# Attention, soft MoE and FFN in one kernel: four more half loads of v, a second feature tile converted early, five unused products

## The chip, the cores and the metric

One core of one Trainium2 chip runs the whole program in a single launch. The metric is the device time of one execution in microseconds (us), the median of several runs.

## The reference

Three layers follow each other. The first is windowed attention over 4 batches, 8 heads, 576 positions of 64 dimensions: the first four heads see the last 32 positions, the others every fourth of the last 128. The second is a soft mixture of 8 experts with 4 slots each, over all 2304 tokens. The third is a feed-forward layer (FFN) of 2048 features with a leaky gate; its weights arrive as 64-bit floats.

```python
scores = np.where(mask, scale * (q @ k.T), -1e9)
x = softmax(scores) @ v                            # then (B*S, H*D) = 2304 x 512
logits = x @ phi                                   # 2304 x 32
slot_input = softmax(logits, axis=0).T @ x         # 32 slots
slot_out[e] = np.maximum(slot_input[e] @ w1[e], 0) @ w2[e]
x = softmax(logits, axis=1) @ slot_out
h = x @ w_in                                       # 2304 x 2048
out = (np.maximum(h, 0) + alpha * np.minimum(h, 0)) @ w_out
```

## The kernel before

**Attention.** A unit is a pair of heads of one batch; there are 16 units (`u`), four for each batch. Each unit has nine blocks of 64 queries, and eight blocks in a row make a group (`g`), so 18 groups run through one pipeline: scores on TensorE (PE) into PSUM (`emit_s`, L360), maximum and subtraction on VectorE (DVE; L371, L374), exp on ScalarE (ACT; L377), sum and reciprocal on DVE, the scaling on GpSimd (POOL; `emit_norm`, L390), a transpose on PE (L395), its eviction by ACT or DVE, the product with v on PE (`emit_pv`, L408) and its eviction into `xt`. Behind it follow the logits (L440), transposes of x (L481) and the partial slot inputs (L490), batch by batch.

**The loads of v.** A block needs 64 keys in two overlapping layouts, so `v_m` holds v twice: rows 32 to 95 hold 64 rows, and rows 0 to 31 and 96 to 127 hold the same data shifted by one block. `load_v` (L332) brings all 128 rows (576 KB), or, for the units in `COPIED`, rows 32 to 95 alone (288 KB). For those, four tasks `vc` (`emit_vc`, L336) copy 32 rows each, on POOL (L342, a product with ones), ACT (L424) or DVE (L426); `emit_pv` of these blocks waits for them.

**Who sets the order.** `tasks_of_attention` (L508) lists the tasks with their needs, and `schedule` (L148) runs a list planner with costs from `COST` 2500 times with shaken keys and keeps the best order; tasks made with `either` may go to several engines. So another set of tasks gives another order on all engines. The FFN is planned in the same way (1500 rounds). Attention's tail (L647 to L695) and the experts (L816 to L853) are written out by hand.

**Loads.** All large loads are issued by SyncE (SP) in program order; a load waits for its place to be free, and what is behind it waits too. `plan` (L233) lists the loads of the expert weights (`a` for w1, `b` for w2, 1 or 2 MB each) and of the FFN's feature tiles; `order` (L216) names the place of each. Twelve places of 1 MB (`w0` to `w11`) are free from the start and are filled during attention. The next ones are `q_m`, `ep_m` and `v_m`, attention's own buffers, which come free when its scores (`q_m`) or its last product with v (`ep_m`) are done. After that each pair of places is loaded again when an expert has used it. Of feature tile 0, `w_in`'s half (`i`, 512 KB) is loaded ahead of the last expert's second matrix, and `w_out`'s half (`o`) behind it; feature tiles 1 to 15 (`f`) are loaded whole, 1 MB each.

**Feature tiles.** A tile is 128 features: 512 columns of w_in and 512 of w_out, as pairs of 32-bit words. `conv` (L789) makes a 32-bit float of each pair: step 0 on ACT (L796), steps 1 to 4 on DVE (L798, L800, L803, L806), then w_out is split into a high part (step 5, L424 or L426) and a low part (step 6, L813). Tile 0's w_in half is converted during the experts (L845), its w_out half as tasks `d0` to `d4` of the FFN; tiles 1 to 15 are converted whole as tasks `c0` to `c6`.

**The FFN.** `m1` and `m2` (L901, L978) multiply the slots' output with w_in, ACT (`ms`, `mp`) and DVE (`m3`, L906) make `mpack` of it; `h_` (L912) multiplies it with the packed softmax of the tokens (`cpack`), 384 tokens at a time. Then ACT takes relu (L1016), DVE the gate (L920), ACT the high part (`ghs`), POOL the low part (`gls`, L1022), and PE three products into `y` (L926): high by high, low weight by high, high by low. `VISITS` (L32) orders the work over three ranges of 768 tokens so that few features are needed at first: range 0 with feature 0, range 1 with features 0 and 1, range 2 with 0 to 2, and so on. After each visit ACT or DVE evicts six tiles of `y`.

`warm` (L503) issues products that nobody reads; `st` is the transposed output of the experts, `soT` its copy.

## Time and profile before

| what | us |
|---|---|
| median of 3 runs | 379.26 (378.06 to 381.27) |
| the profiled execution | 377.96 |
| its span, first to last instruction | 376.2 |
| PE, DVE, ACT, POOL busy | 357.4, 264.2, 216.6, 158.3 |

Everything that is read from a trace belongs to the profiled execution. Its time exceeds its span by 1.76 us, and the median of the runs lies 1.30 us above it. Attention's products end at 86 us, its tail at 94.7, the experts at 134, and the FFN's first product into `y` starts at 142.7. A busy PE is not PE at its peak, since matmuls overlap and their ends are modelled.

### The profile page before, as it was taken

To read this page: it belongs to the slowest core of one execution; us is meant where nothing else is said; L and a number is where in the kernel's file an instruction comes from. 1 tells how busy PE (TensorE), PEld (TensorE's weight loads), DVE (VectorE), ACT (ScalarE), POOL (GpSimd) and SP (SyncE) were. 2 spreads that over 40 slices of the span, in tenths; PEclk is the share of its full clock that TensorE was granted. 3 is DMA by queue.
4 is the path that set the end of the run, shared out by engine and by line. 5 is a ranking of instruction groups with operands and counts; after the bars stand their busy time and mean duration, and the time that the engine had idled before them with its cause. 6 is when DMAs were issued, how large, how long until landed. Compare 5 with 4: busy or idle time off the path is not lost.

```text
span 376.2 us, 7864 instructions
## 1 busy us (share of the span) xinstructions
PE 357.4 (95%) x3103; PEld 267.9 (71%) x3104; DVE 264.2 (70%) x455; ACT 216.6 (58%) x467; POOL 158.3 (42%) x145
## 2 busy tenths in 40 slices
PE   8699999998999878899999999999999999999995
PEld 3577777865444255677778778888888877888884
DVE  4979889875167349999999989898885224224263
ACT  2578969663122249878784956656556445535450
POOL 8336645320000005635655456574636424633550
PEclk9999999999999999999999999999999999999999
DMA  7999999999999993332333333110000000003246
GB/s 279 406 420 404 367 400 401 413 419 426 425 427 421 412 426 159 112 113 112 112 114 112 112 113 112 37 77 0 3 1 1 2 0 0 2 0 113 56 142 193
DMA packets 14036, 73.74 MB, mean 196 GB/s; under 512 B 1936, under 2 KB 2592, under 8 KB 9136
## 3 DMA queue, kind: packets, MB, share of 16 engines
q1 hardware_dynamic: 12736, 71.80, 48.7%
q10 hardware_dynamic: 1200, 1.38, 1.1%
q8 instruction: 24, 0.39, 0.4%
q14 instruction: 12, 0.10, 0.1%
q0 software_dynamic: 64, 0.07, 0.1%
HBM read 68.53 MB, written 4.72 MB: 195 GB/s over the span
## 4 chain that ended last, share of the span: by engine, by line
PE 71%; DMA 12%; DVE 8%; ACT 3%; POOL 2%; issue 2%; SPq 0%; DVEq 0%; POOLq 0%; ACTq 0%
PE y L926 45%; DMA w<-w 6%; PE pv L408 4%; PE hb L912 4%; PE s L360 3%; PE x L481 2%; PE si L490 2%; DMA v_m<-v 2%; PE h L724 2%; DMA q_m<-qk 2%; PE t L395 2%; DVE ep_m L803 2%; PE o L746 2%; PE lt L440 1%; DVE gs L920 1%
## 5 line engine op out<-in xcount | busy, mean ns | idle before, releaser
L1022 POOL TENSOR_TENSOR gls<-gs,ghs 128x384 fp32r<-128x384 f32 x96 | 116.0, 1223 | 162.9 <-ACT ghs L424 112.1
L926 PE MATMUL y<-wo_hi,ghs 128*128 128x512 f32 x289 | 90.8, 398 | 1.1 <-ACT ghs L424 0.9
L920 DVE SCALAR_TENSOR_TENSOR gs<-gs,beta_s,hb 128x384 f32<-128x384 f32 x96 | 56.4, 609 | 49.2 <-ACT gs L1016 45.8
L926 PE MATMUL y<-wo_hi,gls 128*128 128x512 f32 x289 | 87.5, 392 | 1.0 <-POOL gls L1022 1.0
L926 PE MATMUL y<-wo_lo,ghs 128*128 128x512 f32 x289 | 88.4, 392 | 0.0
L1016 ACT ACTIVATE gs<-hb 128x384 f32<-128x384 f32 x96 | 44.8, 494 | 45.5 <-PE hb L912 39.0
L926 PEld LDWEIGHTS y<-wo_hi,gls 128*128 128x128 f32 x289 | 54.1, 188 | 13.0 <-POOL gls L1022 1.7
L926 PEld LDWEIGHTS y<-wo_hi,ghs 128*128 128x128 f32 x289 | 53.3, 188 | 13.5 <-ACT ghs L424 2.4
L424 ACT CAST ghs<-gs 128x384 fp32r<-128x384 f32 x96 | 48.9, 517 | 22.5 <-DVE gs L920 21.8
L926 PEld LDWEIGHTS y<-wo_lo,ghs 128*128 128x128 f32 x289 | 54.0, 188 | 10.3
L390 POOL TENSOR_TENSOR ep_m<-ep_m,l 128x512 f32<-128x512 f32 x18 | 19.0, 1063 | 31.0 <-DVE l L386 16.2
L912 PE MATMUL hb<-cpack,mpack 128*128 128x384 f32 x96 | 29.2, 341 | 1.7 <-DVE mpack L906 1.1
L798 DVE TENSOR_SCALAR ep_m<-ep_m 128x1024 f32<-128x1024 f32 (+1 forms) x17 | 18.0, 1059 | 10.4 <-ACT ep_m L796 10.4
L360 PE MATMUL s<-q_m 128*64 128x64 f32 x576 | 20.8, 224 | 2.1 <-DVE l L381 1.5
L360 PEld LDWEIGHTS s<-q_m 128*64 128x64 f32 x576 | 18.6, 138 | 5.8 <-ACT q_m L424 2.9
L912 PEld LDWEIGHTS hb<-cpack,mpack 128*128 128x128 f32 x96 | 17.9, 188 | 6.3 <-DVE mpack L906 1.3
L408 PE MATMUL pv<-ep_m,v_m 128*64 128x64 f32 x576 | 20.2, 224 | 0.1
L424 ACT COPY ep_m<-t 64x512 f32<-64x512 f32 x34 | 19.7, 580 | 0.9 <-PE t L395 0.3
L408 PEld LDWEIGHTS pv<-ep_m,v_m 128*64 128x64 f32 x576 | 18.2, 138 | 2.7 <-issue 2.3
L800 DVE TENSOR_SCALAR ep_m<-ep_m 128x1024 int32<-128x1024 int32 (+1 forms) x17 | 16.7, 984 | 0.2
L727 ACT ACTIVATE v_m<-h,rinv 128x256 f32<-128x256 f32 x8 | 3.8, 474 | 20.7 <-PE h L724 20.7
L377 ACT ACTIVATE ep_m<-ep_m 128x512 f32<-128x512 f32 x18 | 11.4, 631 | 7.6 <-DVE ep_m L374 7.3
(149 smaller groups left out, 490.7 us busy)
## 6 DMA issues: line engine op xcount, KB each, us to landing
w<-w SPq DMA_DIRECT2D x14, 1024.0 KB, 8.6
w<-w SPq DMA_DIRECT2D x5, 2048.0 KB, 15.5
q_m<-qk SPq DMA_DIRECT2D x13, 576.0 KB, 6.6
q_m<-w_f SPq DMA_DIRECT2D x7, 1024.0 KB, 4.9
v_m<-w_f SPq DMA_DIRECT2D x7, 1024.0 KB, 4.8
v_m<-v SPq DMA_DIRECT2D x12, 576.0 KB, 6.7
q_m<-w SPq DMA_DIRECT2D x2, 2048.0 KB, 15.0
ep_m<-w SPq DMA_DIRECT2D x1, 2048.0 KB, 10.0
```

The source lines that it names most:

```text
L360: mm(s[r:r + 64, col:col + 64], lhsT=q_of(u)[:, 2 * o:2 * o + 64], rhs=keys(u, c, x), start=False, stop=True, skip_group_check=True)
L377: nc.scalar.activation(out=es[g % 4], in_=es[g % 4], func=AF.Exp, scale=SCALE)
L390: nc.gpsimd.tensor_tensor(out=e, in0=e, in1=bc(e_[g, "l"], 128, 8, 64), op=ALU.mult)
L408: mm(pv[hs, n], lhsT=vv[u % 4][:, c, hs], rhs=pts[:, NBS * (g % 2) + n, h], start=True, stop=True, skip_group_check=True)
L424: nc.scalar.copy(out=out, in_=in_)
L798: nc.vector.tensor_scalar(out=t, in0=t, scalar1=2.0 ** -15, scalar2=FMAX, op0=ALU.max, op1=ALU.min)
L800: nc.vector.tensor_scalar(out=ti, in0=ti, scalar1=3, scalar2=0x3FFFFFFF, op0=ALU.logical_shift_left, op1=ALU.bitwise_and)
L912: mm(hb[i], lhsT=mpack[:, 128 * f:128 * f + 128], rhs=cpack[:, t0:t0 + 384], start=True, stop=True)
L920: nc.vector.scalar_tensor_tensor(out=g, in0=g, scalar=beta_s[:, f:f + 1], in1=hb[i], op0=ALU.mult, op1=ALU.add)
L926: mm(y[steps[s][0], t][:, sl], lhsT=g, rhs=wo_hl[p == 1][:, f, sl], start=start, stop=stop, skip_group_check=True)
L1016: lambda s=s, i=i: nc.scalar.activation(out=half(gs, s, i, 4), in_=hb[i], func=AF.Relu, scale=-1.0),
L1022: lambda s=s, i=i: nc.gpsimd.tensor_tensor(out=half(gls, s, i, 6), in0=half(gs, s, i, 4), in1=half(ghs, s, i, 6).bitcast(F32), op=ALU.subt ...
```

## The change

Eight units instead of four (3, 4, 6, 7, 8, 10, 11, 12) load rows 32 to 95 of v and have the other rows copied: 16 more copies, four more loads of 288 KB in the place of 576 KB. Feature tile 1 is treated like tile 0: its w_in half (512 KB) is loaded ahead of the last expert's second matrix, into `xs`, and converted during the experts, its w_out half is loaded behind that matrix and converted in the FFN by the half-size steps. Three calls of `warm` in attention's tail issue five products that nobody reads.

```diff
--- before.py
+++ after.py
@@ -58,10 +58,11 @@
             c6=14, warm=60, pb=8)
 NST = HP * NC // 2
 NQ, NXT = 4, 7
-COPIED = (4, 6, 8, 10)
+COPIED = (3, 4, 6, 7, 8, 10, 11, 12)
 QZ = 2 * S
 KP = 2 * S + WIN
 NW = 12
+EARLY = (0, 1)
 
 
 def constants():
@@ -213,7 +214,7 @@
     slots = {"xs": xs_m[:, 0:2048]}
     for n, m in pairs.items():
         slots.update({n: m[:, 0:2048], second[n]: m[:, 2048:]})
-    order = [f"w{i}" for i in range(NW)] + ["q0", "q2", "e", "v0"] + ["w0", "w2", "w4", "w6", "w8", "q0", "w10", "w11", "q0", "xs", "q3", "v0", "v1"] + 3 * ["q2", "q3", "v0", "v1"]
+    order = [f"w{i}" for i in range(NW)] + ["q0", "q2", "e", "v0"] + ["w0", "w2", "w4", "w6", "w8", "q0", "xs", "w10", "w11", "q0", "xs", "q3", "v0", "v1"] + 3 * ["q2", "q3", "v0", "v1"]
 
     eye_s = const.tile([128, 128], F32, name="eye_s")
     sel_s = const.tile([128, 128], F32, name="sel_s")
@@ -235,9 +236,9 @@
         plan += [("a", e, x) for x in ((0, 1) if e < 4 else (2,))]
         if e > 0:
             plan += [("b", e - 1, x) for x in ((0, 1) if e < 3 else (2,))]
-    plan += [("i", 0, 0), ("b", NE - 1, 0), ("b", NE - 1, 1), ("o", 0, 0)]
-    FB = len(plan) - 1
-    plan += [("f", c, 0) for c in range(1, NF)]
+    plan += [("i", f, 0) for f in EARLY] + [("b", NE - 1, x) for x in range(2)]
+    FB = len(plan)
+    plan += [("o" if f in EARLY else "f", f, 0) for f in range(NF)]
     wt = {}
 
     def load_one(i):
@@ -664,6 +665,7 @@
         emit_dexp(b)
         x_(2, "act")
         emit_dT(b)
+        warm(2, tail[3][:, 128:256])
         emit_dTe(b)
         g1, g2 = small("g1", 1, 96), small("g2", 1, NS)
         nc.vector.tensor_reduce(out=g2, in_=j1[0:1, 0:96].rearrange("p (j s) -> p s j", j=3), op=ALU.min, axis=AX.X)
@@ -672,6 +674,7 @@
         emit_lts(b)
         emit_lrun(b)
         emit_part(b, 0)
+        warm(1, tail[3][:, 128:256])
         j2 = tail[1]
         mm(j2[0:96, 0:1], lhsT=g1, rhs=one_s, start=True, stop=True)
         gm, fac, lf = small("gm", 96, 1), small("fac", 96, 1), small("lf", 96, 1)
@@ -684,6 +687,7 @@
         emit_acc(b)
         j3 = tail[2]
         mm(j3[:, 0:1], lhsT=sel_s[0:96, :], rhs=lf, start=True, stop=True)
+        warm(2, tail[3][:, 128:256])
         used["xs"] = True
         load_weights()
         j4 = tail[3]
@@ -842,8 +846,9 @@
 
         yacc = [part(q_m, i, DM) for i in range(7)] + [part(xs_m, i, DM) for i in range(6)]
         yacc += [acc_m, v_m[:, 4096:4608]] + [part(m_m, i, DM) for i in range(3)]
-        for i in range(5):
-            conv(0, i, 0)
+        for f in EARLY:
+            for i in range(5):
+                conv(f, i, 0)
         emit_l2(NE - 1, 1)
         nc.scalar.copy(out=os, in_=o)
         warm(2, st[:, 256:384])
@@ -960,19 +965,14 @@
 
         for f in range(NF):
             k = when[f]
-            if f > 0:
-                landed = [("c4", x) for x in NEXT if NEXT[x] == f and x > 0]
-                for i in range(7):
-                    need = {0: landed + [dep("c6", f - 4), dep("m1", f - 4)], 5: [("c4", f)], 6: [("c5", f)]}
-                    task((f"c{i}", f), "act" if i in (0, 5) else "dve", lambda f=f, i=i: conv(f, i),
-                         need.get(i, [(f"c{i - 1}", f)]), k - LEAD[f"c{i}"], f"c{i}",
-                         2.6 * f + 1.6 if f < 6 else 0.0)
-            else:
-                for i in range(5):
-                    task((f"d{i}", 0), "dve" if i else "act", lambda i=i: conv(0, i, 1), [dep(f"d{i - 1}", 0)], -40, f"d{i}")
-                task(("c5", 0), "dve", lambda: conv(0, 5), [("d4", 0)], -40, "c5")
-                task(("c6", 0), "dve", lambda: conv(0, 6), [("c5", 0)], -2, "c6", 3.0)
-            task(("m1", f), "pe", lambda f=f: m1(f), [dep("c4", f), dep("ms", f - 1)], k - LEAD["m1"])
+            early = f in EARLY
+            landed = [("c4", x) for x in NEXT if NEXT[x] == f and x > 0] + [dep("c6", f - 4), dep("m1", f - 4)] if not early else []
+            for i in range(7):
+                kind = f"d{i}" if early and i < 5 else f"c{i}"
+                task((f"c{i}", f), "act" if i == 0 or i == 5 and f else "dve", lambda f=f, i=i: conv(f, i, 1 if f in EARLY and i < 5 else None),
+                     [(f"c{i - 1}", f)] if i else landed, (-40, -2)[i > 5] if f == 0 else k - LEAD[f"c{i}"], kind,
+                     3.0 if (i, f) == (6, 0) else 0.0 if early else 2.6 * f + (0 if 1 in EARLY else 1.6) if f < 6 else 0.0)
+            task(("m1", f), "pe", lambda f=f: m1(f), [None if f in EARLY else ("c4", f), dep("ms", f - 1)], k - LEAD["m1"])
             task(("ms", f), "act", lambda f=f: copy("act", ms[:, f % 2], mb[0]), [("m1", f), dep("m2", f - 2)],
                  k - LEAD["ms"])
             task(("m2", f), "pe", lambda f=f: mm(mb[1], lhsT=sel_s, rhs=ms[:, f % 2], start=True, stop=True),
```

On SP, at the end of attention and in the experts, the loads stand as follows before (w_84 is the pair of places w10 and w11, which takes the last expert's second matrix).

```order
L251 DMA q_m<-w 128x4096 x2
L251 DMA ep_m<-w 128x4096
L251 DMA v_m<-w 128x4096
L251 DMA w_79<-w 128x4096
L251 DMA w_80<-w 128x4096
L251 DMA w_81<-w 128x4096
L251 DMA w_82<-w 128x4096
L251 DMA w_83<-w 128x4096
L247 DMA q_m<-w_f 128x1024
L251 DMA w_84<-w 128x2048 x2
L247 DMA q_m<-w_f 128x1024
L247 DMA xs_m<-w_f 128x2048
```

Now:

```order
L252 DMA v_m<-w 128x4096
L252 DMA w_79<-w 128x4096
L252 DMA w_80<-w 128x4096
L252 DMA w_81<-w 128x4096
L252 DMA w_82<-w 128x4096
L252 DMA w_83<-w 128x4096
L248 DMA q_m<-w_f 128x1024
L248 DMA xs_m<-w_f 128x1024
L252 DMA w_84<-w 128x2048 x2
L248 DMA q_m<-w_f 128x1024
L248 DMA xs_m<-w_f 128x1024
L248 DMA q_m<-w_f 128x2048
```

The load of tile 1's w_in (into xs_m) has moved ahead of the two loads into w_84, and its w_out stands alone behind tile 0's.

On POOL, in the middle of attention, copies of v (L342) and the scaling of a group (L390) stand as follows before.

```order
L390 TENSOR_TENSOR ep_m<-ep_m,l 128x512 x5
L342 TENSOR_TENSOR v_m<-v_m,ones_s 32x512
L342 TENSOR_TENSOR v_m<-v_m,ones_s 32x640
L342 TENSOR_TENSOR v_m<-v_m,ones_s 32x512
L390 TENSOR_TENSOR ep_m<-ep_m,l 128x512 x3
L342 TENSOR_TENSOR v_m<-v_m,ones_s 32x512 x2
L342 TENSOR_TENSOR v_m<-v_m,ones_s 32x640
L342 TENSOR_TENSOR v_m<-v_m,ones_s 32x512
L390 TENSOR_TENSOR ep_m<-ep_m,l 128x512 x2
L342 TENSOR_TENSOR v_m<-v_m,ones_s 32x512
L390 TENSOR_TENSOR ep_m<-ep_m,l 128x512
```

Now (L343 is the copy, L391 the scaling, L328 a copy of q):

```order
L391 TENSOR_TENSOR ep_m<-ep_m,l 128x512 x2
L343 TENSOR_TENSOR v_m<-v_m,ones_s 32x512 x2
L391 TENSOR_TENSOR ep_m<-ep_m,l 128x512
L343 TENSOR_TENSOR v_m<-v_m,ones_s 32x512
L328 TENSOR_TENSOR q_m<-q_m,ones_s 64x18x32
L391 TENSOR_TENSOR ep_m<-ep_m,l 128x512
L343 TENSOR_TENSOR v_m<-v_m,ones_s 32x640
L343 TENSOR_TENSOR v_m<-v_m,ones_s 32x512 x4
L391 TENSOR_TENSOR ep_m<-ep_m,l 128x512 x2
L343 TENSOR_TENSOR v_m<-v_m,ones_s 32x512
L343 TENSOR_TENSOR v_m<-v_m,ones_s 32x640
L343 TENSOR_TENSOR v_m<-v_m,ones_s 32x512
```

Between two scalings there are now up to five copies in a row, where there were up to four, and nearly every gap holds one. In all of attention POOL has 22 copies of v in place of 11, ACT 10 in place of 3, DVE none in place of 2.

On ACT, from the copy of the experts' output (soT) to the first high part (ghs), the rows stand as follows before.

```order
L852 COPY soT_93<-st_1904 128x128
L796 ACTIVATE ep_m_69<-q_m_67 128x512
L424 COPY q_m_67<-hb0_1949 128x128
L424 CAST mpack_1939<-hb1_1950 128x128
L796 ACTIVATE ep_m_69<-xs_m_70 128x1024
L1016 ACTIVATE gs_1940<-hb0_1949 128x384
L1016 ACTIVATE gs_1940<-hb1_1950 128x384
L796 ACTIVATE ep_m_69<-q_m_67 128x1024
L424 CAST ghs_1941<-gs_1940 128x384
```

Now:

```order
L857 COPY soT_93<-st_1927 128x128
L800 ACTIVATE ep_m_69<-xs_m_70 128x512
L800 ACTIVATE ep_m_69<-q_m_67 128x512
L425 COPY q_m_67<-hb0_1977 128x128
L425 CAST mpack_1967<-hb1_1978 128x128
L425 COPY q_m_67<-hb0_1977 128x128
L1016 ACTIVATE gs_1968<-hb1_1978 128x384
L800 ACTIVATE ep_m_69<-q_m_67 128x1024
L1016 ACTIVATE gs_1968<-hb0_1977 128x384
L425 CAST ghs_1969<-gs_1968 128x384
L425 CAST wo_hi_1965<-ep_m_69 128x512
L425 CAST ghs_1969<-gs_1968 128x384
```

Two half-size steps 0 (tile 1's from xs_m, tile 0's from q_m) now stand ahead of the first copy of `hb0`, where one stood, and tile 1's own copy of `hb0` has moved ahead of the first relu; the whole step 0 of tile 1 (xs_m, 128x1024) is gone.

## Rows read from the trace of the kernel before

**Rows 1.** The windows view: stretch, its length, busy us of each engine, clock, DMA share, GB/s.
```profile
0.00:30.00 30.00, 24.51 (x402) 17.00 (x403) 22.51 (x57) 15.36 (x27) 15.29 (x23) 1.00 0.95 371
30.00:60.00 30.00, 29.29 (x577) 23.25 (x576) 26.45 (x61) 25.36 (x55) 19.18 (x19) 1.00 1.00 387
60.00:84.00 24.00, 23.48 (x407) 17.61 (x405) 20.27 (x53) 17.68 (x43) 7.33 (x8) 1.00 1.02 416
...
88.00:94.70 6.70, 5.51 (x44) 3.09 (x45) 3.49 (x15) 2.19 (x7) 0.00 (x0) 1.00 1.01 419
...
142.70:156.00 13.30, 11.36 (x54) 8.20 (x54) 12.54 (x18) 12.50 (x25) 7.61 (x6) 1.00 0.15 65
...
200.00:376.00 176.00, 172.28 (x839) 140.49 (x837) 110.99 (x159) 94.98 (x204) 82.86 (x72) 1.00 0.17 57
...
24.00:28.00 4.00, 3.69 (x103) 3.15 (x102) 2.35 (x6) 3.04 (x7) 0.95 (x1) 1.00 1.02 419
```

**Rows 2.** The chain that ended last: start us, us, what.
```profile
21.86 7.31 DMA v_m<-v
...
30.41 2.26 POOL v_m L342 x2
...
109.85 22.84 DMA w<-w
132.73 1.11 PE o L746 x8
```

**Rows 3.** DMA issues: out<-in, queue, count, KB of one, median us to landing.
```profile
q_m<-w SPq DMA_DIRECT2D x2, 2048.0 KB, 15.0
...
v_m<-v SPq DMA_DIRECT2D x12, 576.0 KB, 6.7
...
ep_m<-w SPq DMA_DIRECT2D x1, 2048.0 KB, 10.0
...
v_m<-v SPq DMA_DIRECT2D x4, 288.0 KB, 6.9
```

**Rows 4.** SP's timeline: start us, length, issue.
```profile
73.62 0.83 SPq L251 DMA_DIRECT2D q_m<-w  x2
86.80 0.33 SPq L251 DMA_DIRECT2D ep_m<-w  x1
...
96.64 9.17 SPq L251 DMA_DIRECT2D w<-w  x5
```

**Rows 5.** The DMA view of 155:159 in 40 slices, one load issued at 155.10.
```profile
GB/s 0 0 0 0 0 0 0 0 0 0 410 246 0 0 0 0 0 164 164 328 82 573 573 164 573 573 164 492 573 246 492 573 246 492 573 164 573 573 164 573
```

**Rows 6.** The tile view of w: what ended PE's idle time before its products.
```profile
  DMA w<-w: 4.9, 3
```

**Rows 7.** The groups by line, kept apart by shape.
```profile
L342 POOL TENSOR_TENSOR v_m<-v_m,ones_s 32x512 f32<-32x512 f32 x8 | 8.3, 1036 | 4.0 <-DMA v_m<-v 3.9
...
L426 DVE COPY q_m<-q_m 64x576 f32<-64x576 f32 x11 | 6.0, 548 | 3.2 <-DMA q_m<-qk 3.0
...
L426 DVE COPY v_m<-v_m 32x512 f32<-32x512 f32 x2 | 1.9, 942 | 0.1
...
L506 PE MATMUL st<-eye_s 128*128 128x128 f32 x8 | 1.4, 298 | 0.0
...
L806 DVE SCALAR_TENSOR_TENSOR ep_m<-q_m,ep_m 128x512 int32<-128x512 int32 x2 | 1.4, 692 | 0.1
...
L796 ACT ACTIVATE ep_m<-q_m 128x512 f32<-128x512 f32 x2 | 1.4, 688 | 0.0
...
L800 DVE TENSOR_SCALAR ep_m<-ep_m 128x512 int32<-128x512 int32 x2 | 0.9, 426 | 0.1
```

**Rows 8.** The timeline of attention's tail: start us, busy us, instructions, idle before.
```profile
90.30 1.06 PE L490 MATMUL si<-xs_m,dT 96*32 96x512 f32 x6 [0.54 <-ACT fb L460]
```

**Rows 9.** The timeline of the FFN's head, with the same columns.
```profile
136.14 0.27 ACT L852 COPY soT<-st 128x128 f32<-128x128 f32 x1 [1.69 <-PE st L506]
...
142.71 0.96 PE L926 MATMUL y<-wo_hi,ghs 128*128 128x512 f32 x3
```

## The prediction

> **What bounds the kernel now.** I read three views in this order: the windows, stage by stage (columns: PE, its weight loads, DVE, ACT, POOL), the chain of waits, and the DMA issues with SP's timeline. In attention's middle the reader is to see PE as the limit: 29.29 of 30 us and 23.48 of 24 us, 0.71 + 0.52 = 1.23 us idle between 30 and 84 us. Only the first 30 us leave PE 5.5 us idle. At the same time the DMA share is 0.95 to 1.02, so the loads are full as well [rows 1]. The chain goes through v where data is scarce: unit 4's half load ends at 21.86 + 7.31 = 29.2 us, and two of its copies on POOL (2.26 us) stand behind it. Of the four units that are copied, this is the only one whose copies appear so. The experts end on a load of w that lands at 109.85 + 22.84 = 132.7 us, and PE's products follow at once [rows 2]; PE sat idle for loads of w three times, 4.9 us in all [rows 6]. So two limits run side by side up to 86.8 us, and up to 132.7 us the stream of loads alone is the limit. In the FFN's head, from 142.7 to 156 us, ACT (12.50 of 13.30 us) and DVE (12.54) are both full while PE has 1.94 us idle. From 200 us on PE is busy in 172.28 of 176 us [rows 1].
>
> The granted clock is 1.00 in all these stretches, which is the upper level of 2.4 GHz, the tail included (88 to 94.7 us) [rows 1]. The five products therefore have no clock to win back.
>
> **A. Attention.** Four units bring 288 KB less, 0.295 MB each. The rate in 24 to 28 us, when unit 4's half load is on its way, is 419 GB/s [rows 1], so a half load saves 0.295 MB / 419 GB/s = 0.70 us of the stream. Only unit 3's stands ahead of the stretch in which PE is short of data, so unit 4's data comes 0.70 us earlier. Against it stand unit 3's own copies; one takes 1.04 us on POOL [rows 7], and POOL has half of the first 30 us free [rows 1]. I take -0.4 us, near the middle of -0.7 and 0. The best end is -1.9 us (0.70 and all of PE's 1.23 us). The worst is +2.26 us for each new unit whose two POOL copies enter the chain as unit 4's did [rows 2]; the others stand in a stretch with PE full and POOL busy for 19.18 of 30 us, then 7.33 of 24 us [rows 1], so I take none of them.
>
> **B. The stream of loads.** All four units take 4 x 0.70 = 2.8 us out of it. How much of that survives depends on the queue at the point where SP next waits: ep_m, issued at 86.80 us after attention's last product with v [rows 4]. It lands 10.0 us after its issue [rows 3]. 2 MB at 419 to 425 GB/s are 4.9 us, and a load in an idle queue has a fixed part: the one issued at 155.10 us moves its first data in slices 11 and 12 (156.1 us) and runs evenly from slice 18 on (156.7 to 156.9 us) [rows 5], 1.0 to 1.6 us. So what stood ahead of ep_m was between 10.0 - 4.9 - 2.4 = 2.7 us (with 1.5 us for the start and 0.9 us for its end) and 10.0 - 4.9 - 0.9 = 4.2 us (the start hidden behind the queue). The two loads into q_m, issued at 73.62 us and landing after 15.0 us in the median [rows 3, 4], are that queue. I take the middle, 3.4 us: the old queue is empty at 90.2 us. With 2.8 us less data it would be empty at 87.4 us, but the issue itself comes only 0.4 us earlier (A), at 86.4 us, and its data 1.5 us later, at 87.9 us. 0.5 us is lost, **2.3 us survive** (bounds: 1.6 us with 2.7 us of queue, 2.8 us with 4.2 us). The next wait of SP is at 96.64 us [rows 4] with two 2 MB loads issued ahead of it; the issue of 96.2 us brings data at 97.7 us, and the stream would be empty at 90.2 + 9.8 - 2.3 = 97.7 us: nothing is lost there.
>
> The other way, tile 1's w_in half (512 KB = 0.524 MB, 1.25 us at 419 GB/s) now stands ahead of the last expert's second matrix, which is what the chain waits for at 132.7 us. **+1.25 us.** The experts' end moves by -2.3 + 1.25 = -1.05 us.
>
> **C. Five products.** A product of this kind takes 0.298 us [rows 7], five 1.5 us; PE has 6.70 - 5.51 = 1.19 us idle in the tail [rows 1], 0.54 us of it in one place, ahead of si [rows 8]. Their cost on PE is between 0 and 1.5 us. I take 0.2 us and put it at nothing, since PE then waits 4.9 us for w [rows 6]. Without that cover it would be 0.2 us, and at the dear end SP's issue at 96.64 us would come late and cost up to 1.5 us of stream.
>
> **D. The FFN's head.** Tile 1's half of step 0 leaves ACT there (0.688 us), and its half of steps 1 to 4 leaves DVE (2 x 0.426 + 2 x 0.692 = 2.24 us) [rows 7]. That work goes into the experts, where the chain waits for DMA. But what is left of both tiles stands nearer to the front: ACT now does two half steps 0 between soT and the first copy of hb0, where one stood, so the first product into y may start later than the 6.57 us that it starts after soT now (136.14 to 142.71 us) [rows 9]. Both engines are full up to 156 us, so the smaller relief decides: between 0 and 0.69 us, and I take **-0.3 us**. The bounds are -2.2 us (DVE alone was the limit) and +2.2 us (tile 1's second half delays the first gate by as much and nothing is won back).
>
> **E. The FFN's body** gets another order from the planner. PE has 176 - 172.28 = 3.7 us idle there [rows 1]; I put the difference at 0, with 1 us to each side as an estimate from that remainder.
>
> **The sum:** -1.05 + 0 - 0.3 + 0 = -1.35 us against the execution's 377.96 us gives 376.6 us. The median of the runs shown lies 1.30 us above the execution, so the forecast of the median is **377.9 us**. Attention's own -0.4 us is in B already, since the stream decides when the experts end.
>
> **The rivals.** *Everything survives.* If attention ends 0.9 us earlier or more, because the early loads fill some of PE's 5.5 idle us, ep_m's data is there at 87.4 us and all of 2.8 us stays: -2.8 + 1.25 = -1.55 us; if DVE alone bounds the head, -2.24 us more. 377.96 - 3.8 = 374.2 us, median **375.5 us**. For it speaks the idle PE early on; against it the full ACT in the head. Chance 0.20.
>
> *Copies in attention's chain* (the other side). POOL does 22 copies where it did 11, in rows of up to five (5.2 us) between two scalings that PE's transposes wait for. If the copies of three of the four new units end last, attention ends 3 x 2.26 - 0.7 = 6.1 us later; ep_m's data then starts at 86.8 + 6.1 + 1.5 = 94.4 us, 4.2 us after the old queue's end, and nothing of the 2.8 us is left: +4.2 + 1.25 - 0.3 = 5.1 us, median **384.4 us**. With two units it is 2.9 us (382.2 us), and from the third on it is over 1%. For it speaks unit 4's row in the chain, against it the free POOL. It may also come by way of DVE: a DVE copy of v took 942 ns beside POOL's, though a copy of more columns (64x576) takes 548 ns [rows 7]. If each of 11 more POOL copies held DVE for 1.04 us, 11.4 us would meet DVE's free 3.55 + 3.73 = 7.3 us between 30 and 84 us [rows 1]: attention 4.1 us later, about 382 us. But DVE's own two copies go away. Chance of all of this 0.09.
>
> The Trainium skill, "SBUF — State Buffer", section "Who interferes with whom", says that GpSimd shares a pair of ports with VectorE and that whoever comes second is blocked for the whole instruction, for those DVE operations that use the second port; ACT and PE never wait. By that rule the 942 ns would be a blocked copy and the 382 us way is the one to fear; the row of 942 ns is the only sign of it in this trace.
>
> *A half load takes as long as a whole one.* Its landing says so at first sight: 6.9 us against 6.7 us [rows 3]. Against it speaks the rate of 419 GB/s while one was on its way [rows 1]; in a full queue the landing tells of the queue. Then nothing is saved: +1.25 - 0.3 = 0.95 us, median **380.2 us**. Chance 0.11.
>
> **How the numbers follow.** The forecast has 0.60; its own range is 376.3 to 379.5 us (survival of 1.6 to 2.8 us, head and body by about 1 us). The range with the rivals is 374.7 to 381.0 us: below, the first rival with a body 0.8 us better; above, the third with 0.8 us more; beyond it lie the copies in the chain. About 1% (3.8 us) is what a measurement of this kernel can tell from no change. Faster by more than that is half of the first rival and the lower rest of the forecast, 0.10 + 0.08 = 0.18. Slower by more is the greater part of the second, 0.06. The rest is 0.76.
>
> **What would show it.** ep_m's load is issued at about 86.4 us; the first product with the last b starts about 1 us before 132.7 us; PE's wait for w is near 4.9 us less what the tail took. No copy of v is in the chain between 30 and 86 us except unit 4's or unit 3's. soT to the first y takes longer than 6.57 us, but 156 us and what follows come about 1.4 us earlier. The prediction is wrong if attention's last product moves by more than 1 us, if the last load of w lands later than before, or if the FFN from the first y on differs by more than 1 us.

## The result and the profile after

| | us |
|---|---|
| changed kernel, median of 19 runs | 384.06 (380.42 to 388.40) |
| kernel before, median of 19 runs beside it | 380.64 (378.06 to 381.98) |
| ratio | 1.0082, 95% interval 1.0059 to 1.0106 |
| the profiled execution of the changed kernel, its span | 384.89, 383.1 |

The change made the kernel 0.8% (3.1 us) slower, where 377.9 us and a range of 374.7 to 381.0 us were forecast. It is inside the 1% that was called the bound of what can be told from no change, and the interval still excludes 1.000. About 1.4 us of the distance to the forecast is its base: the kernel before has a median of 380.64 us over 19 runs, and the forecast started from 379.26 us, the median of 3. Ratios and mean clocks leave out the few runs that lie more than 1.5% above the fastest of their kernel.

The windows view of the changed kernel, with the columns and stretches of [rows 1] and, at the experts' end, slices of 1 us:

```profile
0.00:30.00 30.00, 24.94 (x389) 17.60 (x391) 23.82 (x54) 17.52 (x33) 17.21 (x26) 0.94 0.96 376
30.00:60.00 30.00, 29.06 (x591) 23.23 (x588) 28.99 (x61) 23.83 (x53) 22.93 (x22) 1.00 0.99 382
60.00:84.00 24.00, 20.90 (x376) 16.76 (x374) 18.86 (x45) 17.60 (x40) 11.62 (x12) 0.93 0.96 368
88.00:94.70 6.70, 6.58 (x116) 5.51 (x111) 3.76 (x9) 3.10 (x9) 0.50 (x1) 1.00 0.78 265
138.00:139.00 1.00, 0.00 (x0) 0.00 (x0) 0.89 (x2) 0.00 (x0) 0.00 (x0) 0.87 1.03 422
139.00:140.00 1.00, 0.79 (x4) 0.20 (x8) 0.00 (x0) 0.00 (x0) 0.00 (x0) 0.50 1.07 446
140.00:141.00 1.00, 1.00 (x8) 0.00 (x0) 0.00 (x0) 0.00 (x0) 0.00 (x0) 0.50 1.02 422
142.00:143.00 1.00, 1.00 (x11) 1.00 (x9) 0.00 (x0) 0.00 (x0) 0.00 (x0) 0.92 0.98 410
142.70:156.00 13.30, 11.67 (x78) 8.93 (x77) 11.23 (x19) 10.47 (x22) 4.47 (x4) 1.00 0.48 198
200.00:376.00 176.00, 176.00 (x852) 143.27 (x851) 115.97 (x161) 98.23 (x212) 87.74 (x76) 1.00 0.16 55
```

The mean clock of this execution is 0.987. It was 1.00 throughout in the execution read before [rows 1]; now it is 0.94 in the first 30 us and 0.93 in 60 to 84 us, and at the experts' end it is 0.50, the lower level of 1.2 GHz, from 139 to 141 us and on. PE is idle for 3.1 us in 60 to 84 us where it was for 0.52 us. The loads, full before, run at 265 GB/s (share 0.78) in 88 to 94.7 us, against 419: that is the hole in the stream that part B of the prediction warned of, but of about 2.5 us (an estimate, 6.7 us x (1 - 265/419)) where B lost 0.5 us. From 200 us on PE is never idle.

SP's timeline of the changed kernel, the issues that answer to [rows 4]:

```profile
77.79 1.14 SPq L252 DMA_DIRECT2D q_m<-w  x2
90.41 0.33 SPq L252 DMA_DIRECT2D ep_m<-w  x1
...
102.04 9.18 SPq L252 DMA_DIRECT2D w<-w  x5
```

ep_m's load is issued 3.6 us later than before (90.41 against 86.80), not 0.4 us earlier, and the five loads of w 5.4 us later. Two rows of the chain of waits answer to [rows 2], the load that the experts' end hangs on and the products behind it:

```profile
115.72 23.44 DMA w<-w
139.21 1.94 PE o L750 x8
```

PE's timeline tells what these products waited for. The kernel before, then the changed one (start us, busy us, instructions, idle before):

```profile
130.33 1.07 PE L746 MATMUL o<-w,hT 128*32 128x512 f32 x8 [1.32 <-DMA w<-w]
132.73 1.06 PE L746 MATMUL o<-w,hT 128*32 128x512 f32 x8 [1.33 <-DMA w<-w]
```

```profile
136.78 1.06 PE L750 MATMUL o<-w,hT 128*32 128x512 f32 x8 [2.38 <-DMA w<-w]
139.21 1.94 PE L750 MATMUL o<-w,hT 128*32 128x512 f32 x8 [1.37 <-DMA w<-w]
```

PE's wait for the first half of the last matrix has grown from 1.32 to 2.38 us, by 1.06 us, near the 1.25 us that the prediction gave the 512 KB ahead of it. Then the eight products of the second half take 1.94 us instead of 1.06: PE did the same work at the lower clock. In the FFN's head the rows that answer to [rows 9] are:

```profile
143.67 0.27 ACT L857 COPY soT<-st 128x128 f32<-128x128 f32 x1 [1.87 <-PE st L507]
...
151.13 1.19 PE L931 MATMUL y<-wo_hi,ghs 128*128 128x512 f32 x4 [0.18 <-ACT ghs L425]
```

From soT to the first product into y it is 7.46 us (6.57 before), and from soT to the end of the span 239.4 us (383.1 - 143.67) where it was 240.1: the FFN begins later and ends relatively earlier, as forecast. So the whole loss lies before soT, which comes 7.5 us later in this pair of executions. This pair overstates the loss, as the runs below show.

### The profile page after: what moved, and what is told of

The parts are those of the page before. It is cut to its first block, busy times and chain, and to the rows that moved or that the text cites. A ratio compares the mean times of both kernels' runs of the same rounds, so it can differ in the third digit from the quotient of the medians.

```text
span 383.1 us, 7903 instructions
## 1 busy us (share of the span) xinstructions
PE 362.2 (95%) x3114; PEld 272.7 (71%) x3114; DVE 270.1 (71%) x458; ACT 219.1 (57%) x475; POOL 167.8 (44%) x156
## 4 chain that ended last, share of the span: by engine, by line
PE 74%; DMA 8%; ACT 7%; DVE 6%; issue 2%; POOL 1%; SPq 0%; DVEq 0%
PE y L931 50%; DMA w<-w 6%; PE hb L917 4%; PE s L361 3%; DMA v_m<-v 2%; PE pv L409 2%; PE x L482 2%; PE h L728 2%; PE o L750 2%; PE si L491 1%; ACT ep_m L425 1%; PE hb L906 1%; PE d L621 1%; PE lt L441 1%; PE t L396 1%
## 5 line engine op out<-in xcount | busy, mean ns | idle before, releaser
L1022 POOL TENSOR_TENSOR gls<-gs,ghs 128x384 fp32r<-128x384 f32 x96 | 114.3, 1205 | 164.5 <-ACT ghs L425 112.2
L1016 ACT ACTIVATE gs<-hb 128x384 f32<-128x384 f32 x96 | 45.7, 496 | 37.7 <-PE hb L917 31.5
L391 POOL TENSOR_TENSOR ep_m<-ep_m,l 128x512 f32<-128x512 f32 x18 | 19.0, 1059 | 26.9 <-DVE l L387 11.6
L917 PE MATMUL hb<-cpack,mpack 128*128 128x384 f32 x96 | 30.4, 347 | 0.2 <-DVE gs L925 0.2
L343 POOL TENSOR_TENSOR v_m<-v_m,ones_s 32x512 f32<-32x512 f32 (+1 forms) x22 | 24.0, 1096 | 3.7 <-DMA v_m<-v 2.5
L361 PE MATMUL s<-q_m 128*64 128x64 f32 x576 | 22.6, 233 | 2.3 <-issue 1.9
L361 PEld LDWEIGHTS s<-q_m 128*64 128x64 f32 x576 | 19.9, 145 | 6.5 <-issue 5.7
L802 DVE TENSOR_SCALAR ep_m<-ep_m 128x1024 f32<-128x1024 f32 (+1 forms) x18 | 16.4, 916 | 9.7 <-ACT ep_m L800 9.6
L750 PE MATMUL o<-w,hT 128*32 128x512 f32 x96 | 13.6, 640 | 3.7 <-DMA w<-w 3.7
L817 DVE TENSOR_TENSOR wo_lo<-ep_m,wo_hi 128x512 fp32r<-128x512 f32 x16 | 16.5, 1031 | 0.2 <-ACT wo_hi L425 0.2
```

Of the source, the lines that this page charges most:

```text
L343: nc.gpsimd.tensor_tensor(out=w[o:o + 32, a:b], in0=w[r:r + 32, a - d:b - d], in1=ones_s[r:r + 32].to_broadcast([32, b - a]), op=ALU.mult)
L361: mm(s[r:r + 64, col:col + 64], lhsT=q_of(u)[:, 2 * o:2 * o + 64], rhs=keys(u, c, x), start=False, stop=True, skip_group_check=True)
L391: nc.gpsimd.tensor_tensor(out=e, in0=e, in1=bc(e_[g, "l"], 128, 8, 64), op=ALU.mult)
L750: mm(o[32 * g:32 * g + 32, :], lhsT=ht[:, 4 * r + g, 28 - 4 * e:60 - 4 * e], rhs=w[:, g, :], start=(e == 0 and r == 0), stop=(e == NE - 1 ...
L817: nc.vector.tensor_tensor(out=wo_hl[1][:, f, :], in0=t[:, 512:], in1=wo_hl[0][:, f, :].bitcast(F32), op=ALU.subtract)
L917: mm(hb[i], lhsT=mpack[:, 128 * f:128 * f + 128], rhs=cpack[:, t0:t0 + 384], start=True, stop=True)
```

## The experiments

Each kernel was timed against the kernel before on the same chip, in 12 runs (19 of the change, 11 of early_only, 6 of copied_s2 and copied_nopool). The table gives the ratio with its 95% interval, the mean of the granted clock over the kernel's runs, and from one profiled execution of each the start of the experts' first product (h) and of the second half of the last expert's second matrix (o), both from PE's timeline.

| kernel | ratio | clock | h, o (us) |
|---|---|---|---|
| before_again | 0.9993 (0.9958 to 1.0028) | 0.994 | 96.78, 135.30 |
| warm_only | 1.0009 (0.9977 to 1.0041) | 0.994 | 95.71, 133.45 |
| early_only | 1.0077 (1.0051 to 1.0104) | 0.984 | 97.72, 137.59 |
| whole0_ahead | 1.0051 (1.0023 to 1.0080) | 0.988 | 98.15, 137.51 |
| i1_behind | 1.0029 (0.9995 to 1.0062) | 0.994 | 99.39, 136.22 |
| after_fill | 1.0063 (1.0036 to 1.0089) | 0.997 | 97.39, 138.08 |
| after_fill8 | 1.0050 (1.0024 to 1.0076) | 0.997 | 98.69, 137.39 |
| the change | 1.0082 (1.0059 to 1.0106) | 0.989 | 100.05, 139.21 |
| copied_only | 1.0021 (0.9992 to 1.0051) | 0.995 | 99.43, 136.58 |
| whole_copied | 1.0086 (1.0054 to 1.0117) | 0.991 | 100.12, 138.31 |
| copied_x | 1.0052 (1.0030 to 1.0075) | 0.994 | 99.95, 137.25 |
| copied_s2 | 1.0103 (1.0079 to 1.0127) | 0.994 | 101.05, 141.09 |
| copied_nopool | 1.0181 (1.0147 to 1.0214) | 0.991 | 103.31, 140.42 |
| copied_noeps | 1.0013 (0.9986 to 1.0040) | 0.993 | 99.78, 137.70 |
| before_noeps | 1.0003 (0.9975 to 1.0031) | 0.995 | 95.38, 134.44 |
| before_fill | 0.9986 (0.9958 to 1.0014) | 0.996 | 95.03, 135.96 |
| before_fill4 | 0.9978 (0.9952 to 1.0004) | 0.995 | 95.54, 133.79 |
| best | 0.9983 (0.9958 to 1.0008) | 0.997 | 95.35, 133.74 |
| best_noeps | 0.9974 (0.9949 to 0.9998) | 0.997 | 95.83, 134.70 |

**The parts alone.** The kernel before once more:

> The kernel before, run as one of its own, to see whether its profile and clock repeat. Theory A (attention with eight copied units runs in a worse order and ends later): the last product with v of before ends near 86.2 us again, no idle of PE over 1.3 us between 30 and 84 us, clock near 1.00, ratio 1.000. Rival B (a hole without a visible releaser on PE and the clock that falls behind it are chance, and any execution can have them): one of them shows here too, and the clock of single runs lies between 0.98 and 1.00 as after the change.

It repeated in time but not in its profile: span 380.3 us, clock 0.991, its o products at 1.94 us too. Of 34 runs of the kernel before beside it, 3 had a mean clock of 1.000 and 30 had 0.995 or less. The low clock is no property of the change; the execution that the prediction was read from was one of the few without it. Rival B holds so far: single executions scatter.

> The change with EARLY and the five products undone; eight copied units stay. Theory A: nearly all of the loss is here, ratio 1.007 to 1.011; attention's last product with v ends at 89 to 90 us and the stream of loads has a gap at the issue into ep_m. Rival C (the loss is tile 1's w_in ahead of the last expert's second matrix): the ratio is 0.993 to 1.000, as 2.3 us of loads are saved. Rival B: about 1.000, with a scatter as wide as after the change.

```diff
-EARLY = (0, 1)
+EARLY = (0,)
-    ... "w8", "q0", "xs", "w10", "w11", "q0", "xs", ...
+    ... "w8", "q0", "w10", "w11", "q0", "xs", ...
-        warm(2, tail[3][:, 128:256])
...
```

1.0021, at most 1.0051 by its interval: the loss as a whole is not here, as theory A had it. In its profile attention does end later, with the gap in the stream, but most of it does not reach the end.

> EARLY = (0, 1) alone, with four copied units and no products. Theory A: 1.25 us later at the experts' end, 0.3 to 2 us won in the FFN's head, ratio 0.998 to 1.003. Rival C: ratio 1.006 or more, with a wait for the last w over 2 us and a low clock behind it.

```diff
-COPIED = (3, 4, 6, 7, 8, 10, 11, 12)
+COPIED = (4, 6, 8, 10)
-        warm(2, tail[3][:, 128:256])
...
```

1.0077: nearly all of the loss, as rival C said, with a wait of 2.57 us, the o products at 1.94 us and the lowest clock of all kernels:

```profile
135.17 1.29 PE L747 MATMUL o<-w,hT 128*32 128x512 f32 x8 [2.57 <-DMA w<-w]
137.59 1.94 PE L747 MATMUL o<-w,hT 128*32 128x512 f32 x8 [1.12 <-DMA w<-w]
```

> The five products alone. Theory A and rival C alike: nothing, ratio 0.999 to 1.001, attention's tail 0 to 0.4 us longer, PE's wait for w shorter by as much. If they keep the clock up behind the tail in some executions, the ratio is 0.998.

```diff
         emit_dT(b)
+        warm(2, tail[3][:, 128:256])
         emit_dTe(b)
...
```

1.0009, and the clock is not raised: the five products cost and bring nothing that can be measured in time. In the trace they make attention's tail 0.43 us longer (8.86 us instead of 8.43 from the end of the last product with v to h).

**Is it the load or the FFN's order?** Two kernels tell the load from what else EARLY does.

> The kernel before with tile 0 loaded whole (1 MB) where its w_in half (512 KB) was loaded, ahead of the last expert's second matrix: 512 KB more ahead of it, as in the change, and nothing else moved (the FFN's order is the one before). Theory C (the 512 KB ahead of the last expert's second matrix are the loss): PE's single longest wait for w grows from 1.3 to about 2.5 us, the granted clock falls behind it in most executions, ratio 1.005 to 1.008. Rival D (the loss is the FFN's head, whose first product into y comes 7.8 instead of 6.57 us after soT): ratio 0.999 to 1.004, 1.25 us at most.

```diff
...
-    plan += [("i", 0, 0), ("b", NE - 1, 0), ("b", NE - 1, 1), ("o", 0, 0)]
+    plan += [("f", 0, 0), ("b", NE - 1, 0), ("b", NE - 1, 1)]
```

1.0051 with the FFN of before: 512 KB ahead of the last matrix cost 1.9 us, and the mean clock falls to 0.988. In its one profile the waits were 0.91 and 1.35 us and the clock stayed up behind them, so the longer wait that was expected was not seen there; the ratio and the clock of its 12 runs are what carries this.

> The change with tile 1's w_in loaded behind the last expert's second matrix instead of ahead of it, and converted after the last product of the experts. Theory C: the wait for w is back at 1.3 us and the clock's mean at 0.993; what is left are the eight copied units, ratio 1.000 to 1.003. Rival D: 1.006 to 1.009, as the FFN's head keeps its new order.

```diff
...
-    plan += [("i", f, 0) for f in EARLY] + [("b", NE - 1, x) for x in range(2)]
+    plan += [("i", 0, 0)] + [("b", NE - 1, x) for x in range(2)] + [("i", 1, 0)]
...
         nc.scalar.copy(out=os, in_=o)
+        for i in range(5):
+            conv(1, i, 0)
```

With the same load (and its conversion) behind the last matrix the change is at 1.0029 and its clock at 0.994. From both sides the load's place is worth 0.5% (0.0051, and 1.0082 - 1.0029 = 0.0053), 2.0 us, give or take 0.3 to 0.4% by the intervals. Rival D falls: the loss is there with the FFN of before as well, and the FFN itself takes less time after the change, as is shown under D below.

**The clock's share.** Products that nobody reads fill PE's waits for w.

> The changed kernel with 14 and 8 products that nobody reads ahead of the products of the last expert's second matrix, in PE's waits for w. If the low clock behind those waits is part of the loss: no low clock at 136 to 143 us, the products of the last matrix take 1.06 us instead of 1.94, the mean clock of the runs rises to 0.992 or more, ratio 1.001 to 1.004. If the loss is the loads' 1.25 us alone: ratio stays at 1.007 to 1.009.

> The kernel before with 8 and 8 such products in the same two waits of 1.3 us. If the clock theory holds: the mean clock rises from 0.9925 toward 0.996, ratio 0.995 to 0.999. If the clock falls elsewhere (attention's start, attention's middle): 1.000.

The edit of before_fill; after_fill has 14 in place of the first 8:

```diff
                 st = ps_2.tile([128, 512], F32, tag="t", name="st")
+                warm(8, st[:, 256:384])
...
+        warm(8, st[:, 256:384])
         emit_l2(NE - 1, 1)
```

The clock rose to 0.997 and 0.996, but both fills were too long: a call of 14 products is 28 records and 3.39 us in the trace, so PE came to the weights late. They were halved, to 8 and 4 in the changed kernel and 4 and 4 in the one before:

> The changed kernel with 8 and 4 products in its waits of 2.4 and 1.4 us (14 and 8 put the last product 1.5 us later). Clock theory: mean clock 0.996, the last product of the experts 39.2 us behind their first instead of 40.7, ratio 1.001 to 1.004. If the loss is not the clock: 1.006 or more.

> The kernel before with 4 and 4 products in the two waits of 1.3 us (8 and 8 were twice as long as the waits and put the last product of the experts 2.4 us later). Clock theory: no delay now, mean clock 0.996, ratio 0.994 to 0.998. If the low clock of the executions comes from elsewhere: 0.999 to 1.001.

```profile
134.99 1.06 PE L750 MATMUL o<-w,hT 128*32 128x512 f32 x8
...
137.39 1.06 PE L750 MATMUL o<-w,hT 128*32 128x512 f32 x8 [0.26 <-DMA w<-w]
...
140.81 0.27 ACT L859 COPY soT<-st 128x128 f32<-128x128 f32 x1 [1.69 <-PE st L507]
```

These are rows of after_fill8. The wait shrinks to 0.26 us, the products run at 1.06 us, no run of either kernel has a mean clock under 0.99. With nothing changed but these products the mean clock rises from 0.989 to 0.997, so most of what the change lost of it was lost at these two waits. From the start of that last half to soT it is 3.42 us here and 3.41 us in the execution before, but 4.46 us in the change's, 4.61 in before_again's and 5.68 in early_only's: the low clock costs 1.0 to 2.3 us in an execution in which it falls there. The ratio of the changed kernel goes from 1.0082 to 1.0050, 0.3% (1.2 us) for the clock. By the intervals this difference is 0.32% give or take 0.35%, so in time alone it is not clear of nothing; and 1.0050 is short of the 1.001 to 1.004 that was expected. In the kernel before the gain of 0.2% is not clear of 1.000 either.

**Why eight copied units don't save.** The loads and the copies are priced apart, then the order and the engines.

> The eight copied units alone, in the same order on every engine, but units 3, 7, 11 and 12 load all rows of v again (576 KB), so their copies write what has been loaded already: the price of the copies without the saved 1.2 MB. Against copied_only (1.0021): if the saved loads are worth 2.3 to 2.8 us there, 1.008 to 1.010; if they are worth nothing because attention ends later and the queue runs dry anyway, 1.001 to 1.004.

```diff
-        r = slice(32, 96) if u in COPIED else slice(0, 128)
+        r = slice(32, 96) if u in (4, 6, 8, 10) else slice(0, 128)
```

With the copies but without the saved loads it is 1.0086. So the four half loads are worth 0.0086 - 0.0021 = 0.65% (2.5 us, give or take 1.6 us by the intervals), close to the 2.3 us of part B, and the 16 copies with the order they bring cost 0.86% (3.3 us, give or take 1.2 us). The gain is there, and the copies take more than it.

> The eight copied units alone, with the last three transposes of x of batch 3's first pair forced ahead of the last product with v, as the kernel before has them. If the order is the loss of the eight units (transposes behind the last product, 1.35 us): from that product to the experts' first 8.4 us instead of 9.8, ratio 0.997 to 1.000. If it is the copies themselves: the last product with v comes later by as much, ratio 1.002 to 1.004 again.

```diff
-                 + [("vc", u, int(c > 4), i) for _, u, c in blocks(g) for i in range(2)], k + 8.0)
+                 + [("vc", u, int(c > 4), i) for _, u, c in blocks(g) for i in range(2)]
+                 + [("x", B - 1, 0, m) for m in range(3) if g == NG - 1], k + 8.0)
```

In copied_only the last transposes of x stand behind the last product with v, where they stood ahead of it. The kernel before, then copied_only:

```profile
82.69 1.52 PE L481 MATMUL x<-eye_s,xt 128*96 128x128 f32 x12
84.14 2.08 PE L408 MATMUL pv<-ep_m,v_m 128*64 128x64 f32 x64
86.15 1.53 PE L440 MATMUL lt<-xt,phi_s 128*32 128x192 f32 x24
...
94.65 2.80 PE L724 MATMUL h<-w,slotT 128*32 128x256 f32 x48 [0.20 <-DVE rinv L694]
```

```profile
87.56 2.09 PE L409 MATMUL pv<-ep_m,v_m 128*64 128x64 f32 x64
89.58 1.51 PE L482 MATMUL x<-eye_s,xt 128*96 128x128 f32 x12
91.02 1.50 PE L441 MATMUL lt<-xt,phi_s 128*32 128x192 f32 x24
...
99.43 2.80 PE L725 MATMUL h<-w,slotT 128*32 128x256 f32 x48 [0.20 <-DVE rinv L695]
```

Forced ahead of it they take 1.35 us out of the tail (8.43 us from the last product with v to h instead of 9.78), but that product ends 1.9 us later in the profile (91.5 against 89.6 us), and the ratio is 1.0052, not better. Moving that step back does not win the loss back.

> The eight copied units alone, with another seed for the order of attention, nothing else. If the eight units' cost is that one order's (13 transposes and evictions behind the last product with v): from that product to the experts' first another time than 9.8 us, ratio off from 1.0021 by more than 0.004, toward 0.996. If it is the copies' own: 1.001 to 1.006, as with the order of copied_x (1.0052).

```diff
-    rng, succ = random.Random(1), {n: [] for n in tasks}
+    rng, succ = random.Random(seed), {n: [] for n in tasks}
...
-                 rounds=ROUNDS, counts=lambda name: name[0] != "w")
+                 rounds=ROUNDS, counts=lambda name: name[0] != "w", seed=2)
```

1.0103 with another seed for attention: three orders of eight copied units lie between 1.002 and 1.010, none below 1. The kernel before was not tried with other seeds, so how far its own order is a good draw stays open.

> The eight copied units alone, with POOL no longer open to the copies of v: all 32 go to ACT and DVE, and the planner finds another order. If POOL's copies are what costs (they block DVE, whose copies of q took 768 ns instead of 548, or stand in the chain): those copies are back at 450 to 560 ns, attention's last product with v ends near 87.5 us, ratio 0.994 to 0.999, as the saved loads are worth 2.5 us. If 16 more copies cost the same on any engine: 1.001 to 1.005.

```diff
-     k + 4.5 + 2.5 * (n > 1), pool=1.15, act=0.66, dve=0.62)
+     k + 4.5 + 2.5 * (n > 1), act=0.66, dve=0.62)
```

1.0181: without POOL it is much worse, though DVE's copies of q were back at 574 ns in the mean (768 in copied_only). 29 of the copies went to ACT, 7 copies of q went to POOL instead, and copies of v on ACT stand for 4.7 us in the chain between 30 and 86 us. It is another order as well, so the run does not price the engine alone; of the kernels tried, those with the copies on POOL were better.

> The eight copied units alone, without the addition of 1e-9 to the sums on DVE (18 of 128x8, 348 ns each there, 176 ns before; the sums are at least 1). Theory P (DVE's operations on two inputs in SBUF and its copies there wait while POOL copies): up to 6.3 us of DVE go from attention's chain, its last product with v comes 1 to 3 us earlier than in copied_only, ratio 0.995 to 1.001; in the mean the reciprocal then still takes 203 ns, as it does not wait for POOL. If PE is the limit and DVE's longer steps are hidden: 1.002 again.

> The kernel before without the same 18 additions (3.2 us of DVE). Theory P: half of the gain of copied_noeps or less, ratio 0.996 to 1.000. If it gains as much as copied_noeps gains over copied_only, the added copies are not what makes the additions dear.

```diff
-        nc.vector.tensor_tensor(out=l, in0=l, in1=eps_s.to_broadcast([128, 8]), op=ALU.add)
         nc.vector.reciprocal(out=l, in_=l)
```

These leave out an addition of 1e-9 to sums that are at least 1. DVE's steps are longer beside POOL's copies: the five additions over 0.7 us in copied_only (0.72 to 0.95 us) all stand beside copies of v on POOL. The tiles l and q_m in the kernel before, then in copied_only (minimum, median and maximum in ns):

```profile
L385 DVE TENSOR_TENSOR l<-l,eps_s x18: 118/156/359, 12.5 to 77.5; 128x8 f32<-128x8 f32 x18
L386 DVE RECIPROCAL l<-l x18: 202/203/205, 12.7 to 77.7; 128x8 f32<-128x8 f32 x18
...
L426 DVE COPY q_m<-q_m x11: 451/458/969, 5.8 to 64.3; 64x576 f32<-64x576 f32 x11
```

```profile
L386 DVE TENSOR_TENSOR l<-l,eps_s x18: 147/168/955, 12.6 to 82.9; 128x8 f32<-128x8 f32 x18
L387 DVE RECIPROCAL l<-l x18: 202/203/205, 12.8 to 83.1; 128x8 f32<-128x8 f32 x18
...
L427 DVE COPY q_m<-q_m x14: 457/590/1510, 5.6 to 67.1; 64x576 f32<-64x576 f32 x14
```

The addition of two inputs from SBUF takes up to 955 ns, a copy in SBUF up to 1510 ns, about the length of POOL's copies, while the reciprocal between them stays at 202 to 205 ns. But 18 additions less make no difference that can be measured (1.0013 against 1.0021, 1.0003 against 1.0000). The intervals leave room for 1.8 us, and that the longer steps are hidden is not shown: in the one profile of copied_noeps DVE's part of the chain between 30 and 86 us falls from 24.3 us (copied_only) to 9.7 us, and loads of q and v, 19.2 us instead of 7.5, take its place.

**A version beside both.** Four copied units, tile 1's w_in behind the last matrix, 4 and 4 products in the waits; then the same without the additions:

> Four copied units and attention as before, no products in attention's tail; tile 1's w_in behind the last expert's second matrix, the FFN in the change's order, and 4 and 4 products that nobody reads in the two waits for w. If the change's FFN is worth 1.5 us or more at full clock and the fill keeps the clock: soT to the end 238 to 239 us, mean clock 0.996, ratio 0.992 to 0.996. If the fill only moves PE's wait and the FFN's gain belongs to eight copied units: 0.998 to 1.001.

> The version with four copied units, tile 1's w_in behind the last matrix and 4 and 4 products in the waits for w (0.9983), without the 18 additions. If the parts add up: 0.994 to 0.998, mean clock 0.996.

0.9983 and 0.9974 (0.9949 to 0.9998). The second is the only kernel here whose interval lies below 1, by 0.0002, which among so many intervals may be chance; taken as it is, it gains 1.0 us on the kernel before. The change's FFN adds nothing clear to before_fill4 (0.9978).

## Why the prediction was wrong, step by step

**The clock** is the first step that failed in the order of the prediction (the largest is A, below): "The granted clock is 1.00 in all these stretches ... The five products therefore have no clock to win back." It was true of the one execution read. Over the runs of the kernel before the mean is 0.993, and PE's waits for the last matrix are one place where it falls. The sum had no term for it. In the changed kernel it is about 1.2 us by the ratio (after_fill8), 1.05 us by the rows from o to soT. Nor is the tail's end free of it: in 4 of the 15 profiles without the five products (whole0_ahead, before_fill, before_noeps, copied_s2) the experts' first 48 records of h take 4.2 to 4.5 us instead of 2.80, and in none of the 5 with them. What that is worth is not shown.

**B, tile 1's load.** The 1.25 us were the right mechanism at the right place, and PE's wait grew by 1.06 us in the change's profile (2.38 against 1.32) and 1.25 in early_only's. As a size it was too small: the load's place costs 2.0 us. The likely rest is the lower clock behind the longer wait, at which the next eight products took 1.94 us instead of 1.06.

**A, attention.** "the others stand in a stretch with PE full and POOL busy for 19.18 of 30 us, then 7.33 of 24 us, so I take none of them". This failed, and it is the largest error: the forecast was 0.4 us earlier, and the copies cost 3.3 us (whole_copied). A free POOL said nothing: PE, DVE and ACT were already at 29.29, 26.45 and 25.36 of 30 us [rows 1], the planner put 10 copies on ACT where 3 were, and moved three more copies of q to DVE. The chain shows what took PE's place. Added up between 30 and 86 us, PE's rows make 28 to 51 us of it and those of DVE and ACT together 2 to 16 us in eight profiles with the attention of before (before, before_again, warm_only, early_only, whole0_ahead, before_fill, before_fill4, best). In six with the eight copied units (the change, after_fill, after_fill8, i1_behind, copied_only, whole_copied) PE's make 11 to 28 us, and those of DVE and ACT 25 to 36 us. The prediction read PE as the limit there from one execution; with the copies DVE and ACT take that place. Rows of the chain after the change:

```profile
39.75 0.75 DVE l L386
...
40.72 0.88 DVE l L386
...
46.38 0.72 ACT v_m L425
...
47.77 0.62 ACT v_m L425
...
52.92 0.73 DVE q_m L427
...
54.68 0.92 DVE q_m L427
```

Two copies of v on ACT stand in it at 46 to 48 us, where the prediction expected none but unit 3's or 4's, and beside them additions and copies of q that are far longer than at their shortest (147 and 457 ns). The tail behind the last product with v is longer by 1.35 us, the moved transposes, in every profile of that order; that product itself ends 1.0 us later in the mean (88.7 us in four profiles of the change's attention, 87.6 us in eight of before's), less than single executions scatter. How the cost divides between ACT's copies, DVE's longer steps and the new order is not told apart by the runs.

**B, what survives of the saved loads.** 2.3 us forecast, 2.5 us (give or take 1.6 us) measured with the order held fixed. The hole in the stream came in the way described, from the later issue, but as attention ended later and not earlier it was about 2.5 us in the change's profile instead of 0.5.

**C** was right in that nothing can be measured in time (1.0009), and its cover is seen in warm_only: the tail is 0.43 us longer where 0.2 us was taken, and PE's wait ahead of the last matrix is 0.99 us instead of 1.32. The 1.5 us of PE's time was near by luck: the five products are ten records (1.82 us by PE's rows in warm_only), and 0.298 us is the length of one record, which overlaps with its neighbours. **D and E** were right within what can be told: 7.46 us instead of 6.57 to the first y, and from soT to the end 0.4 us (early_only) to 1.9 us (after_fill) less than the 240.1 us of before, 0.9 us in the mean of four profiles with the change's FFN (the change, early_only, after_fill, after_fill8), where -0.3 us was forecast. The 13 profiles with the FFN of before lie between 239.9 and 240.4 us, so this gain is there.

So the terms come out as -2.5 + 3.3 + 2.0 - 0.9 = 1.9 us, against 3.1 us measured, where -2.3 + 1.25 - 0.3 = -1.35 us were forecast. Each of the first three is uncertain by more than 1 us, so the sum bears the signs and the order of the terms, not the last microsecond.

**The rivals.** The slower side came by a mixture of the second rival (the copies, less as rows of their own in the chain than as work ahead of others on ACT and DVE) and of a cost that no rival had, the clock behind the load's longer wait. Its way by DVE was seen; what it costs is open. It was to be seen beforehand: the prediction called the 942 ns of a copy of v the only sign, but in the trace before one copy of q took 969 ns and one addition 359 ns, which the mean of 548 ns hides. The Trainium skill, "SBUF — State Buffer", section "Who interferes with whom", says that a DVE operation with two inputs in SBUF, or a copy in a two-port mode, waits while POOL holds the shared pair, and that a reduce does not. The trace agrees on the first two: additions at 147 to 955 ns, copies of q at 457 to 1510 ns. By copied_noeps the additions' share of it is too small to be measured in time; that of the copies of q was not tried alone.

## What to carry to other kernels

Take the clock from the list of all runs before it is called free of loss: one profile may be the lucky one, and a load put ahead of the one that the chain waits for can cost, beside its own time, what PE does at the lower clock behind the longer wait. Where all of PE, ACT and DVE are full, a copy that saves DMA is paid on the engines even if the engine that makes it is half idle; timing the copies with the loads left as they were shows both prices. A transfer that nobody needs soon belongs behind the last one that somebody waits for.

## What the runs showed of the hardware

The same program's attention ended between 86.2 and 89.7 us in eight profiled executions of kernels that are identical up to there (before, before_again, warm_only, early_only, whole0_ahead, before_fill, before_fill4, best): a scatter of 3.5 us, as large as the effects studied here. PE's rate at the lower clock shows in the o products, 1.94 against 1.06 us. A product of 128x128 in 32 bits is two records of about 0.12 us each in a row of many (28 records in 3.39 us), while one record lasts 0.298 us by itself [rows 7], as records overlap. In copied_only the same copy of q on DVE took 457 ns at the least and 1510 ns at the most, an addition 147 and 955 ns. From soT to the end the same FFN took 239.9 to 240.4 us in 13 profiles, so the scatter of these executions comes from what lies ahead of it.
